# Other points in the quads for decoding weights in a fused attention and two-layer MLP kernel

## The chip, the cores and the metric

The kernel runs on one core of a Trainium2 chip. The metric is device time in microseconds (us) of one execution. Engines are named as in the profile: PE is TensorE's matmuls, PEld its weight loads, DVE is VectorE, ACT is ScalarE, POOL is GpSimd, SP is the engine that issues most DMAs.

## The reference, cut to what matters

```python
attn_out = _attn_ref(x, a, B, C)            # chunked linear attention, 4 x 8 x 768 x 32
x = attn_out.transpose(0, 2, 1, 3).reshape(3072, 256)
h = np.maximum(x @ moe_w_in, 0.0);   x = h * h @ moe_w_out       # layer 1: 256 -> 2048 -> 256
h = x @ moe2_w_in                                                # layer 2: 256 -> 2048 -> 256
out = (h * np.clip(h + 3.0, 0.0, 6.0) / 6.0) @ moe2_w_out
```

All in float32.

## The kernel before

**Numbers.** TensorE multiplies operands of a reduced width (float32r). So every float32 operand is kept as a high part, which ScalarE rounds off, and a low part, the rest, which VectorE or GpSimd subtracts; each product is three matmuls (high by high, low by high, high by low). The weights arrive as raw bits and are *decoded* in blocks: block j is 128 x 512 numbers, even j from w_in and odd j from w_out; blocks 2q and 2q+1 serve quad q of a layer.

**Stages.** First the attention, with the first layer's tiles 0 to 3 beside it (`step`, which ends at about 229 us). Then come 32 *quads* (`emit(g, prev)`, g = 0 to 31): g = 0 to 7 are the first layer for tiles 4 and 5, g = 8 to 31 the second layer. A quad takes two token tiles and two blocks of 128 hidden units at once with seven products instead of eight (a Strassen scheme): `p1`, `p2`, `p6`, `p7`, `p5`, `p4`, `p3` into the PSUM banks X, V and Z, and sums of four gate inputs c11, c22, c21, c12.

**What one quad does, in order.** ScalarE copies X aside after p1 (`s1`), after p6 (`u2`) and after p7 (`u3`); the next product into X (p6, p7, p4) has to wait for the copy. VectorE adds: c11 = V + s1, c22 = Z + u3 (the *c22 add*), and, after p3 has been added to Z, c12 = Z + u2. p3 writes the bank that the c22 add reads, so PE can't start p3 before the c22 add is done. Then, in the first layer, relu and square: VectorE does c11 and c12 (L764), ScalarE does c22 and c21 (L749 and L756). ScalarE makes each high part (`ghc`, L772), VectorE each low part (`glc`, L775), and PE multiplies them with the second weights (`second`). c11 is used at the end of its own quad; c22, c21 and c12 in the quad behind (`prev`).

**Order.** Each engine works strictly in the order in which the program is written. Between the quads' own steps lie numbered points, `run(1000 + g, point)`, in the order 0, 1, 6, 2, 3, 5, 4 through a quad, at which side jobs are hung by `at(1000 + g, point, job)`. Point 1 stands ahead of p6, 6 behind the high part of c11, 2 behind `u3`, 5 between square of c22 and relu of c21, 4 at the quad's end. The side jobs here:

- `w1.renew(q)`: the first layer's weights of quad q are added up again (`whole`, VectorE L507, tile `wta..s`) and GpSimd forms four sums of them (`sums`, L500). `w1.both(2q)` then makes high parts (ScalarE L537: `ea`, `ah`) and low parts (GpSimd L544: `ea`, `al`). The tile `wta..s` of one quad lies where an earlier one lay: `whole` waits until the earlier one's last low part is done.
- Second-layer block j: E (`early`, ScalarE L477), B (`begin`, VectorE L481 and L486, tile `lowb`), M (`end`: VectorE L491 `wtb`, for even j GpSimd's four sums L500, then SP's DMA of block j + 2), and H, or F and G (`both`, or its two parts: ScalarE L537 `bh`, `eb`, GpSimd L544 `bl`, `eb`).
- The second layer's token operands: s, h, l (`oper_sum` on GpSimd L674, `oper_high` on ScalarE L685, `oper_low` on VectorE L691).

The plan of the second layer is a string per quad: "5M4" is M of block 4 at point 5.

Of the kernel before, what the change touches and what calls it, by code (L numbers as in the profile page):

```python
# [41 lines left out]
NQ = DFF // (2 * P)  # L42
# [36 lines left out]
def attn_mlp_mlp(ctx: ExitStack, tc, a, bT, cT, bK, x, w1i, w1o, w2i, w2o, yT):  # L79
# [352 lines left out]
    class Weights:  # L432
# [21 lines left out]
        def at(self, q, k, i, n=1):  # L454

            if (self.pre, q) in own:
                return own[self.pre, q][k][:, i:i + n]
            if 4 <= i < 7:
                return self.ext[q][:, i - 4 + 3 * (k == "l"):][:, 0:n]
            d = self.hi if k == "h" else self.lo  # L460
            return d[q][:, i - 3 * (i > 6):][:, 0:n]
# [432 lines left out]
    w1 = w["a"] = Weights(w1i, w1o, "a")  # L894
# [124 lines left out]
    for q in range(NQ - 2):  # L1019
        if q:  # L1020
            at(52 + 2 * q, 0, lambda q=q: w1.both(2 * q - 2))
        at(52 + 2 * q, 0, lambda q=q: w1.renew(q))
    at(1000, 1, lambda: w1.both(2 * (NQ - 3)))
    for q in range(NQ - 2, NQ):
        at(1000 + q - 6, 5, lambda q=q: w1.renew(q))
        at(1001 + q - 6, 1, lambda q=q: w1.both(2 * q))

    for j in range(2):  # L1030
# [2 lines left out]
        at(49 + j, 0, lambda j=j: w2.both(j))  # L1033
    does2 = {"E": w2.early, "B": w2.begin, "M": w2.end, "H": w2.both, "F": lambda j: w2.part(j, 0),
             "G": lambda j: w2.part(j, 1)}
    for g, plan in enumerate(("6E2 2B2 5M2", "2E3 2B3 5M3", "2E4 2B4 5M4", "1F2 1G2 6H3 2E5 2B5 5M5",
# [3 lines left out]
        for d in plan.split():  # L1040
            at(1000 + g, int(d[0]), lambda f=does2[d[1]], j=int(d[2:]): f(j))
# [9 lines left out]
    def operands(g, key, plan):  # L1051
        for dg, p, f, n in plan:
            if f == "s" and key == ("b", NPAIR - 1):
                at(g + dg, p, lambda n=n: later(key, n))
                continue
            at(g + dg, p, lambda f={"s": oper_sum, "h": oper_high, "l": oper_low, "L": by_pool}[f], n=n: f(key, n))
# [6 lines left out]
    operands(1000 + NQ, ("b", 0),  # L1063
# [4 lines left out]
    for p in range(1, NPAIR):  # L1068
# [61 lines left out]
```

## Time and profile before

| | us |
|---|---|
| median of 3 runs (569.37 to 570.31) | 570.16 |
| the profiled execution | 569.82 |
| its span, first to last instruction | 568.1 |
| PE busy in the span | 550.0 (97%) |
| DVE busy | 434.5 (76%) |
| ACT busy | 382.1 (67%) |
| POOL busy | 194.2 (34%) |

The granted clock is 1.00 from 40 us to the last slice. To read it: with PE busy nearly throughout, the interesting places are the few at which it isn't. The quads have 45 matmuls each (quad 0 has 39) and a pace of their own, so a quad that is longer than its neighbours shows a loss. A row by stretch gives its length, the busy us and instructions of PE, PEld, DVE, ACT and POOL, the granted clock, the DMA engines' share and GB/s. Quads 0 to 7 start at 228.96, 239.23, 249.49, 259.69, 269.90, 280.11, 290.33 and 302.63 us.

### The profile page before, as it was taken

The numbers are of one execution on the slowest core, as the hardware profiler recorded it, in microseconds if no ns is written. First come the engines' busy times: TensorE is split into PE (matmuls) and PEld (weight loads), VectorE is DVE, ScalarE is ACT, GpSimd is POOL, SyncE is SP. The second block draws the span as 40 slices with busy tenths as digits, with TensorE's granted clock in tenths as the row PEclk, the third lists the DMA queues.
The fourth block names the chain that finished last, engine by engine and source line by source line (L and its number), as shares of the span: only waits on it lengthen the run. The fifth ranks groups of instructions, "written<-read, shape, count | busy, mean of one in ns | idle before, by whom it ended". The sixth has DMA issues, their size and how long they took to land.

```text
span 568.1 us, 10494 instructions
## 1 busy us (share of the span) xinstructions
PE 550.0 (97%) x4110; PEld 441.9 (78%) x4110; DVE 434.5 (76%) x668; ACT 382.1 (67%) x692; POOL 194.2 (34%) x262
## 2 busy tenths in 40 slices
PE   7699999999999999999998999999999999999996
PEld 4466777787877888788887888778888888888884
DVE  8687778665554788897899988988867788776774
ACT  5486878454344666767877977778766678666664
POOL 3464442320000787676786705651001500000000
PEclk9899999999999999999999999999999999999999
DMA  7897444223000200112121112000200000200002
GB/s 210 204 244 178 123 141 120 61 65 103 1 2 1 75 0 2 37 38 70 42 75 38 37 41 71 0 2 0 75 0 2 1 2 0 75 0 1 0 2 74
DMA packets 26481, 31.43 MB, mean 55 GB/s; under 512 B 2144, under 2 KB 21056, under 8 KB 26432
## 3 DMA queue, kind: packets, MB, share of 16 engines
q1 hardware_dynamic: 24528, 29.85, 19.0%
q10 hardware_dynamic: 1904, 0.92, 0.6%
q8 instruction: 32, 0.52, 0.4%
q14 instruction: 17, 0.14, 0.1%
HBM read 27.41 MB, written 3.35 MB: 54 GB/s over the span
## 4 chain that ended last, share of the span: by engine, by line
PE 73%; DVE 8%; POOL 8%; ACT 4%; issue 3%; DMA 3%; SPq 1%; ACTq 0%; POOLq 0%; DVEq 0%
PE y L788 26%; PE X L732 13%; PE ya L616 10%; PE ha L582 10%; PE Z L732 6%; PE V L732 3%; DVE glc L775 2%; DMA ef<-scr 2%; DVE c L741 1%; PE att L363 1%; POOL ea L544 1%; DVE wtb L491 1%; DVE c L766 1%; PE att L331 1%; POOL bc L295 1%
## 5 line engine op out<-in xcount | busy, mean ns | idle before, releaser
L775 DVE TENSOR_TENSOR glc<-c,ghc 128x512 fp32r<-128x512 f32 x128 | 97.1, 765 | 7.9 <-ACT ghc L772 7.1
L772 ACT ACTIVATE ghc<-c 128x512 fp32r<-128x512 f32 x128 | 77.9, 629 | 2.7 <-DVE c L766 1.7
L788 PE MATMUL y<-glc,bh 128*128 128x512 f32 x192 | 75.1, 391 | 0.1
L788 PE MATMUL y<-ghc,bh 128*128 128x512 f32 x192 | 74.8, 390 | 0.0
L788 PE MATMUL y<-ghc,bl 128*128 128x512 f32 x192 | 74.7, 389 | 0.0
L766 DVE SCALAR_TENSOR_TENSOR c<-rc,c 128x512 f32<-128x512 f32 x72 | 52.4, 728 | 21.7 <-ACT rc L752 21.7
L599 DVE TENSOR_TENSOR gla<-ga,gha 128x512 fp32r<-128x512 f32 x64 | 50.0, 781 | 23.7 <-ACT gha L597 23.2
L752 ACT ACTIVATE rc<-c,three 128x512 f32<-128x512 f32 x72 | 51.9, 721 | 23.8 <-DVE c L741 23.8
L597 ACT ACTIVATE gha<-ga 128x512 fp32r<-128x512 f32 x64 | 40.6, 635 | 36.4 <-DVE ga L595 36.0
L589 ACT ACTIVATE ga<-ha 128x512 f32<-128x512 f32 x64 | 37.9, 592 | 32.0 <-PE ha L582 32.0
L741 DVE TENSOR_TENSOR c<-Z,u 128x512 f32<-128x512 f32 x64 | 44.0, 687 | 19.8 <-PE Z L732 19.1
L595 DVE TENSOR_TENSOR ga<-ga,ha 128x512 f32<-128x512 f32 x48 | 32.9, 685 | 33.4 <-ACT ga L589 33.0
L737 ACT COPY u<-X 128x512 f32<-128x512 f32 x64 | 37.5, 586 | 26.3 <-PE X L732 26.1
L616 PE MATMUL ya<-gha,ah 128*128 128x512 f32 x128 | 52.4, 410 | 0.0
L582 PE MATMUL ha<-act_h,ah 128*128 128x512 f32 x128 | 51.0, 400 | 0.4 <-ACT ah L522 0.4
L582 PE MATMUL ha<-act_h,al 128*128 128x512 f32 x128 | 50.9, 399 | 0.4 <-POOL al L524 0.3
L616 PE MATMUL ya<-gha,al 128*128 128x512 f32 x128 | 50.4, 394 | 0.0
L582 PE MATMUL ha<-act_l,ah 128*128 128x512 f32 x128 | 50.1, 393 | 0.0
L616 PE MATMUL ya<-gla,ah 128*128 128x512 f32 x128 | 50.0, 390 | 0.0
L544 POOL TENSOR_TENSOR bl<-wtb,bh 128x256 fp32r<-128x256 f32 (+1 forms) x34 | 30.9, 933 | 43.5 <-ACT bh L537 43.5
L788 PEld LDWEIGHTS y<-glc,bh 128*128 128x128 f32 x192 | 36.0, 188 | 8.9 <-DVE glc L775 1.7
L788 PEld LDWEIGHTS y<-ghc,bh 128*128 128x128 f32 x192 | 36.0, 188 | 7.7 <-ACT ghc L772 0.4
(296 smaller groups left out, 1242.7 us busy)
## 6 DMA issues: line engine op xcount, KB each, us to landing
rawa<-in_w1i SPq DMA_DIRECT2D x8, 512.0 KB
rawa<-in_w1o SPq DMA_DIRECT2D x8, 512.0 KB
rawb<-in_w2i SPq DMA_DIRECT2D x8, 512.0 KB
rawb<-in_w2o SPq DMA_DIRECT2D x8, 512.0 KB
xb<-in_x SPq DMA_DIRECT2D x24, 128.0 KB
ef<-scr SPq DMA_DIRECT2D x10, 256.0 KB
out_yT<-xf SPq DMA_DIRECT2D x10, 256.0 KB
bc<-in_cT SPq DMA_DIRECT2D x6, 256.0 KB
```

The source lines that it names most:

```text
L582: nc.tensor.matmul(out=h, lhsT=wt[fb][:, k, fo * P:fo * P + P], rhs=xt[t][:, k, :], start=i == 0, stop=i == 5)
L589: nc.scalar.activation(out=g, in_=h, func=AF.Relu)
L597: nc.scalar.activation(out=gh, in_=g, func=AF.Copy)
L599: nc.vector.tensor_tensor(out=gl, in0=g, in1=gh.bitcast(F32), op=ALU.subtract)
L616: nc.tensor.matmul(out=ys[m], lhsT=terms[i][0][fb][:, fo, m * P:m * P + P], rhs=terms[i][1], start=first and i == 0, stop=last and i == 2)
L732: nc.tensor.matmul(out=self.ps[bank], lhsT=lhsT, rhs=rhs, start=start and i == 0, stop=stop and i == 2, skip_group_check=True)
L741: nc.vector.tensor_tensor(out=self.sb[c], in0=self.ps[bank], in1=self.sb[n], op=ALU.add)
L752: nc.scalar.activation(out=self.sb["r" + c], in_=src, func=AF.Relu, bias=three)
L766: nc.vector.scalar_tensor_tensor(out=self.sb[c], in0=self.sb["r" + c], scalar=6.0, in1=src, op0=ALU.min, op1=ALU.mult)
L772: nc.scalar.activation(out=self.gh[c], in_=self.sb[c], func=AF.Copy)
L775: nc.vector.tensor_tensor(out=self.gl[c], in0=self.sb[c], in1=self.gh[c].bitcast(F32), op=ALU.subtract)
L788: nc.tensor.matmul(out=ys[t][m], rhs=terms[i][1], lhsT=w[self.pre].at(self.q, terms[i][0], 7 + 2 * (1 - f) + m)[:, 0], start=first and i = ...
```

## The change

The program computes the same; only points are other ones. For the first layer's weights, `both(10)` goes from point 1 of quad 0 to point 5, `renew(6)` from point 5 to 4, and `both(12)` from point 1 of quad 1 to point 6. For the second layer's blocks, E2 and E4 go from point 6 to point 2; blocks 5 to 8 are decoded earlier or at other points; the high parts of b21 and t2 and the low parts of b11 and b21 in quads 5 and 6 change places.

```diff
-    at(1000, 1, lambda: w1.both(2 * (NQ - 3)))
-    for q in range(NQ - 2, NQ):
-        at(1000 + q - 6, 5, lambda q=q: w1.renew(q))
-        at(1001 + q - 6, 1, lambda q=q: w1.both(2 * q))
+    for g, p, f, q in ((0, 5, w1.both, 2 * (NQ - 3)), (0, 4, w1.renew, NQ - 2), (1, 6, w1.both, 2 * (NQ - 2)),
+                       (1, 5, w1.renew, NQ - 1), (2, 1, w1.both, 2 * (NQ - 1))):
+        at(1000 + g, p, lambda f=f, q=q: f(q))
...
-    for g, plan in enumerate(("6E2 2B2 5M2", "2E3 2B3 5M3", "2E4 2B4 5M4", "1F2 1G2 6H3 2E5 2B5 5M5",
-                              "1F4 1G4 6H5 2E6 2B6 5M6", "1E7 1B7 2M7 2E8 6F6 5B8 5M8 4G6", "1H7 6E9 2B9 2F8 5M9 4G8",
+    for g, plan in enumerate(("2E2 2B2 5M2", "2E3 2B3 5M3", "2E4 2B4 5M4 5E5 4B5", "1M5 1F2 1G2 6H3 2B6 4E6",
+                              "1M6 1F4 1G4 6H5 2E7 2B7 5M7", "1F6 1G6 6H7 2E8 2B8 5M8", "1F8 1G8 6E9 2B9 5M9",
...
-             ((-4, 0, "s", "t1"), (-4, 2, "s", "t2"), (-4, 4, "h", "b11"), (-3, 1, "h", "b21"), (-3, 2, "s", "t4"),
-              (-2, 0, "s", "t3"), (-2, 1, "h", "t2"), (-2, 1, "l", "b11"), (-2, 5, "l", "b21"), (-1, 1, "l", "t2"),
+             ((-4, 0, "s", "t1"), (-4, 2, "s", "t2"), (-4, 4, "h", "b11"), (-3, 1, "l", "b11"), (-3, 4, "h", "b21"), (-3, 2, "s", "t4"),
+              (-2, 0, "s", "t3"), (-2, 2, "h", "t2"), (-2, 1, "l", "b21"), (-1, 1, "l", "t2"),
```

ScalarE in quad 0 (s1, u2, u3 are the copies; ea5, ah5 are `both(10)`; oa2b22 a token operand; wtb1 is E2; xf3 the last tile of the stage before). Before:

```order
L737 COPY s10_3038<-X0_3034 128x512
L537 ACTIVATE ea5_3004<-wta5s_3003 128x384
L537 ACTIVATE ah5_1146<-wta5s_3003 128x128
L685 ACTIVATE oa2b22_3058<-xin5_2366 128x512
L737 COPY u20_3063<-X0_3034 128x512
L772 ACTIVATE ghc11_0_3065<-c11_0_3044 128x512
L477 ACTIVATE wtb1_3068<-rawb2_2564 128x512
L628 COPY xf3_3078<-ya3_00_2674 128x512
L628 COPY xf3_3078<-ya3_01_2675 128x512
L737 COPY u30_3084<-X0_3034 128x512
L749 ACTIVATE c22_0_3093<-c22_0_3093 128x512
L756 ACTIVATE c22_0_3093<-c22_0_3093 128x512
```

ScalarE in quad 0 now:

```order
L685 ACTIVATE oa2b22_3053<-xin5_2366 128x512
L737 COPY u20_3058<-X0_3034 128x512
L772 ACTIVATE ghc11_0_3060<-c11_0_3044 128x512
L628 COPY xf3_3071<-ya3_00_2674 128x512
L628 COPY xf3_3071<-ya3_01_2675 128x512
L737 COPY u30_3077<-X0_3034 128x512
L477 ACTIVATE wtb1_3079<-rawb2_2564 128x512
L749 ACTIVATE c22_0_3088<-c22_0_3088 128x512
L756 ACTIVATE c22_0_3088<-c22_0_3088 128x512
L537 ACTIVATE ea5_3004<-wta5s_3003 128x384
L537 ACTIVATE ah5_1146<-wta5s_3003 128x128
L749 ACTIVATE c21_0_3107<-X0_3034 128x512
```

E2 and `both(10)` stand behind all three copies; `both(10)` now stands between the square of c22 and the relu of c21.

GpSimd at the turn of quads 0 and 1 (al5 is the last of `both(10)`; wtb1 the sums of block 2; wta6s those of `renew(6)`). Before:

```order
L544 TENSOR_TENSOR al5_1147<-wta5s_3003,ah5_1146 128x128
L500 TENSOR_TENSOR wta6s_3100<-wta6s_3100 128x128 x4
L500 TENSOR_TENSOR wtb1_3068<-wtb1_3068 128x128 x4
L544 TENSOR_TENSOR ea6_3101<-wta6s_3100,ea6_3101 128x256
L544 TENSOR_TENSOR ea6_3101<-wta6s_3100,ea6_3101 128x128
L544 TENSOR_TENSOR al6_1326<-wta6s_3100,ah6_1325 128x128
```

GpSimd at the same turn now:

```order
L544 TENSOR_TENSOR al5_1147<-wta5s_3003,ah5_1146 128x128
L500 TENSOR_TENSOR wtb1_3079<-wtb1_3079 128x128 x4
L500 TENSOR_TENSOR wta6s_3119<-wta6s_3119 128x128 x4
L544 TENSOR_TENSOR ea6_3120<-wta6s_3119,ea6_3120 128x256
L544 TENSOR_TENSOR ea6_3120<-wta6s_3119,ea6_3120 128x128
L544 TENSOR_TENSOR al6_1326<-wta6s_3119,ah6_1325 128x128
```

The sums of the first layer's weights now stand second, behind those of block 2. On VectorE the step that feeds them, L507 `wta6s`, stood right behind the c22 add of quad 0, and now stands behind that quad's `glc22`.

VectorE from the c12 mult of quad 2 to the c22 add of quad 3 (lowb5 and lowb6 are B of blocks 5 and 6, wtb2 is M of block 5). Before:

```order
L764 SCALAR_TENSOR_TENSOR c12_2_3325<-c12_2_3325 128x512
L741 TENSOR_TENSOR c11_3_3352<-V3_3344,s13_3342 128x512
L775 TENSOR_TENSOR glc21_2_3349<-c21_2_3320,ghc21_2_3348 128x512
L764 SCALAR_TENSOR_TENSOR c11_3_3352<-c11_3_3352 128x512
L775 TENSOR_TENSOR glc12_2_3361<-c12_2_3325,ghc12_2_3360 128x512
L775 TENSOR_TENSOR glc11_3_3381<-c11_3_3352,ghc11_3_3380 128x512
L481 TENSOR_SCALAR lowb5_3399<-rawb5_3218 128x512
L486 TENSOR_SCALAR lowb5_3399<-rawb5_3218 128x512
L741 TENSOR_TENSOR c22_3_3406<-Z3_3402,u33_3396 128x512
L491 SCALAR_TENSOR_TENSOR wtb2_3291<-wtb2_3291,lowb5_3399 128x512
```

VectorE from quad 2 to quad 3 now (B of block 5 stands ahead of the c12 mult):

```order
L481 TENSOR_SCALAR lowb5_3333<-rawb5_3218 128x512
L486 TENSOR_SCALAR lowb5_3333<-rawb5_3218 128x512
L764 SCALAR_TENSOR_TENSOR c12_2_3326<-c12_2_3326 128x512
L741 TENSOR_TENSOR c11_3_3356<-V3_3348,s13_3346 128x512
L775 TENSOR_TENSOR glc21_2_3353<-c21_2_3321,ghc21_2_3352 128x512
L764 SCALAR_TENSOR_TENSOR c11_3_3356<-c11_3_3356 128x512
L491 SCALAR_TENSOR_TENSOR wtb2_3291<-wtb2_3291,lowb5_3333 128x512
L775 TENSOR_TENSOR glc12_2_3365<-c12_2_3326,ghc12_2_3364 128x512
L775 TENSOR_TENSOR glc11_3_3388<-c11_3_3356,ghc11_3_3387 128x512
L481 TENSOR_SCALAR lowb6_3405<-rawb6_3318 128x512
L486 TENSOR_SCALAR lowb6_3405<-rawb6_3318 128x512
L741 TENSOR_TENSOR c22_3_3412<-Z3_3408,u33_3403 128x512
```

Block 5's B and M, of which M stood behind the c22 add of quad 3, now both stand ahead of it, with block 6's B in the place of block 5's.

## Rows read from the trace of the kernel before

**Rows 1.** The page's first line.

```profile
span 568.1 us, 10494 instructions
```

**Rows 2.** Quads 0, 3, 5, 6: stretch, length, then busy time by engine.

```profile
228.96:239.23 10.27, 9.39 (x40) 7.09 (x39) 8.51 (x13) 7.52 (x15) 6.30 (x11) 1.00 0.16 51
...
259.69:269.90 10.21, 10.21 (x46) 8.45 (x45) 8.39 (x12) 7.62 (x15) 7.10 (x8) 1.00 0.16 47
...
280.11:290.33 10.22, 10.22 (x46) 8.45 (x45) 9.93 (x15) 8.79 (x18) 7.50 (x9) 1.00 0.22 63
290.33:302.63 12.30, 10.69 (x47) 8.29 (x45) 12.27 (x15) 8.46 (x16) 11.02 (x12) 1.00 0.25 78
```

**Rows 3.** Timeline of PE: start, length, work, [idle before <- who ended it].

```profile
233.80 0.97 PE L732 MATMUL X<-oa2t,ea 128*128 128x512 f32 x3
...
236.34 0.50 PE L732 MATMUL X<-oa2t,ah 128*128 128x512 f32 x1 [0.88 <-ACT u L737]
...
300.46 0.96 PE L732 MATMUL Z<-oa2b,ea 128*128 128x512 f32 x3 [1.61 <-DVE c L741]
```

**Rows 4.** Timeline of ACT in quad 0.

```profile
232.03 0.53 ACT L537 ACTIVATE ea<-wta5s 128x384 fp32r<-128x384 f32 x1 [1.42 <-POOL wta5s L500]
...
234.18 0.66 ACT L477 ACTIVATE wtb<-rawb 128x512 f32<-128x512 f32 x1
...
235.68 0.60 ACT L737 COPY u<-X 128x512 f32<-128x512 f32 x1
```

**Rows 5.** Timeline of DVE in quads 0 to 2: c22 adds, L507, glc22.

```profile
236.32 0.69 DVE L741 TENSOR_TENSOR c<-Z,u 128x512 f32<-128x512 f32 x1 [0.19 <-ACT u L737]
236.93 0.68 DVE L507 TENSOR_TENSOR wta6s<-ah,al 128x512 f32<-128x512 f32 x1
...
239.37 0.79 DVE L775 TENSOR_TENSOR glc<-c,ghc 128x512 fp32r<-128x512 f32 x1 [0.56 <-ACT ghc L772]
...
246.47 0.67 DVE L741 TENSOR_TENSOR c<-Z,u 128x512 f32<-128x512 f32 x1
...
249.51 0.79 DVE L775 TENSOR_TENSOR glc<-c,ghc 128x512 fp32r<-128x512 f32 x1 [0.51 <-ACT ghc L772]
```

**Rows 6.** Timeline of POOL in quads 0 and 1.

```profile
232.63 1.69 POOL L544 TENSOR_TENSOR ea<-wta5s,ea 128x256 fp32r<-128x256 f32 x2 [0.63 <-ACT ea L537]
...
237.69 2.80 POOL L500 TENSOR_TENSOR wta6s<-wta6s 128x128 f32<-128x128 f32 x4 [2.94 <-DVE wta6s L507]
...
243.59 2.06 POOL L544 TENSOR_TENSOR ea<-wta6s,ea 128x256 fp32r<-128x256 f32 x2
245.62 0.64 POOL L544 TENSOR_TENSOR al<-wta6s,ah 128x128 fp32r<-128x128 f32 x1
```

**Rows 7.** Timeline of DVE from quad 2's c22 add to quad 3's.

```profile
256.02 0.69 DVE L741 TENSOR_TENSOR c<-Z,u 128x512 f32<-128x512 f32 x1
...
259.13 0.89 DVE L775 TENSOR_TENSOR glc<-c,ghc 128x512 fp32r<-128x512 f32 x1
...
261.32 0.69 DVE L741 TENSOR_TENSOR c<-V,s 128x512 f32<-128x512 f32 x1 [0.69 <-PE V L732]
...
263.12 2.38 DVE L775 TENSOR_TENSOR glc<-c,ghc 128x512 fp32r<-128x512 f32 x2
...
266.93 0.66 DVE L741 TENSOR_TENSOR c<-Z,u 128x512 f32<-128x512 f32 x1
```

**Rows 8.** Timeline of DVE: quad 5's glc22 and quad 6's c22 add.

```profile
290.79 0.68 DVE L775 TENSOR_TENSOR glc<-c,ghc 128x512 fp32r<-128x512 f32 x1
...
299.73 0.67 DVE L741 TENSOR_TENSOR c<-Z,u 128x512 f32<-128x512 f32 x1
```

**Rows 9.** Groups by line in quads 0 to 7: xcount, busy, mean ns, idle before.

```profile
L491 DVE SCALAR_TENSOR_TENSOR wtb<-wtb,lowb 128x512 uint32<-128x512 uint32 x8 | 6.3, 785 | 0.1
...
L486 DVE TENSOR_SCALAR lowb<-rawb 128x512 uint16<-128x512 uint16 x9 | 5.9, 658 | 0.3
L481 DVE TENSOR_SCALAR lowb<-rawb 128x512 uint32<-128x512 uint32 x9 | 5.9, 654 | 0.0
```

## The prediction

> **What bounds the kernel now.** I read the busy times by quad first, then PE's timeline where a quad is too long, then the timelines of the engines that PE waits for. A quad of 45 matmuls takes 10.21 us when nothing is late (quads 3 and 5) [rows 2]. PE loses time at two places that the change touches. In quad 0, p4 starts at 236.34 behind 0.88 us of waiting for ScalarE's copy u3 [rows 3]; quad 0 has 39 matmuls, 8.85 us at that pace, and takes 10.27: 1.4 us lost. In quad 6, p3 waits 1.61 us for VectorE's c22 add [rows 3], and the quad takes 12.30: 2.1 us lost [rows 2]. In the first, ScalarE is late because its copies stand behind decoding work; in the second VectorE is, which is busy 12.27 of 12.30 us [rows 2].
>
> So VectorE's order has to be read as a cycle. From one quad's c22 add to its glc22 there is a *gap* of some 3.0 us (246.47 to 249.51 [rows 5], 256.02 to 259.13 [rows 7]): ScalarE must do relu, square, relu of c21 and the high part first, so VectorE can fill the gap with the c12 add, an M or an L507, and would idle else. From glc22 to the next c22 add runs a *row* with no room in it: seven steps of the gates and whatever decoding stands there. In quad 2 to 3 that row takes 7.80 us, 0.69 of it waiting for PE [rows 7]; in quad 5 to 6, with block 9's B and the low part of b11 in it and GpSimd busy 11.02 of 12.30 us beside it, 8.94 [rows 2, 8]. Gap and light row are 10.1 us, PE's quad 10.21: the cycle is nearly full already, and a step put into a row costs PE time, while one in a gap costs nothing.
>
> **The change, part by part.** The sum is made against the profiled execution: 569.82 us, span 568.1 [rows 1]; it lies 0.34 below the median of the three runs, 570.16, and the 1.7 us outside the span stay.
>
> *Quad 0.* E2 (0.66) and `both(10)`, which waited 1.42 us for GpSimd and took ScalarE's time from 232.03 [rows 4], now stand behind u3. Then u3 waits only for p7 (233.80 + 0.97 [rows 3]) and takes 0.60: done at 235.4 instead of 236.3 [rows 4], and a little earlier yet since p7 itself waited for u2. p4 gains 0.9 to 1.1; I take 1.0.
>
> *Quad 1.* What was taken away stands elsewhere. `both(10)` is now between square of c22 and relu of c21, so the gap becomes 3.0 + 0.6 = 3.6 us; with the c22 add at 235.2 (236.32 [rows 5] less 1.1), glc22 starts at 238.9 instead of 239.37. L507 of `wta6s`, which lay in the gap (236.93 [rows 5]), stands behind glc22 and waits there for the last low part of `both(10)`: ScalarE's ea ends at about 237.7, GpSimd needs 1.69 [rows 6] and a small last one, to 239.6 or so. It costs the row 0.6 to 0.9. The row was 7.10 (239.37 to 246.47 [rows 5]), so the c22 add of quad 1 comes at 238.9 + 7.8 = 246.7, against 246.47. GpSimd gives the same: two sets of sums at 2.80 [rows 6] from 239.6 end at 245.2, then ScalarE's high parts of `both(12)` (0.6) and u3 (0.6), which is queued behind them, end at 246.4. PE, 1.0 ahead, waits for both: the gain of quad 0 is gone at p3 of quad 1. Given back: 1.0 (0.7 to 1.4).
>
> *Quad 2.* L507 of `wta7s` waits for GpSimd's al6: high parts from 245.2, then 2.06 and 0.64 [rows 6], that is 248.4. Behind it on VectorE are M3, the c12 add and glc22: 248.4 + 3 x 0.6 = 250.2, against 249.51 [rows 5]. The row behind it was 6.51 (249.51 to 256.02 [rows 5, 7]): c22 add at 256.7 against 256.02. PE's p3 comes 36 matmuls, 8.16 us, behind a quad's start, here 257.65, and the add ends at 257.4: no loss, but VectorE's reserve is gone.
>
> *Quad 3.* E5 lies at point 5: the gap is 3.1 + 0.5 = 3.6, glc22 at 260.3. The row loses its 0.69 of waiting and takes on block 5's B and M beside block 6's B. L481 and L486 average 0.65 and 0.66, L491 0.79 [rows 9]; with the overlap of neighbours I count 1.5 to 2.0 for the three, and take 1.5, since GpSimd rests for a part of it. 260.3 + 7.1 + 1.5 = 268.9 for the c22 add against 266.93 [rows 7], its end 269.55. PE wants p3 at 259.69 + 8.16 = 267.85 [rows 2]: lost 1.7 (1.2 to 2.1).
>
> *Quad 4.* M6 is in the row, but GpSimd has nothing to do until M6 is done, so the steps ahead of it are short. 3.0 + 7.0 to 7.4 against 10.21: lost 0.1 (0 to 0.4). M6's four sums now stand in front of blocks 4 and 5 on GpSimd and push its work about 3 us later, into the next rows.
>
> *Quads 5 and 6.* In quad 5 the row has b11's low part and B8, in quad 6 b21's low part (before in the gap) and B9: the same steps as the row of 8.94 [rows 8]. If GpSimd is as busy, each cycle is 3.0 + 8.94 = 11.95, a loss of 1.75 each, 3.5 together. The other end is the row of quad 2 to 3, 7.1 with one B, and 0.6 for the low part: 10.7 with the gap, with 0.2 to spare from quad 4 a loss of 0.4 for both. GpSimd's queue (M6's sums, blocks 4 to 7, two token sums, M8's sums) is nearer to the first: I take 2.6. Gone is quad 6's loss: 2.1.
>
> The DMAs move with M. SP issues block 4 when block 2 has been read, which is earlier, and block 5 at M3, 10 us ahead of its E5; they cost nothing.
>
> Sum: -1.0 + 1.0 + 1.7 + 0.1 + 2.6 - 2.1 = +2.3 us, 572.1. With every end low -0.9, with every end high +4.4.
>
> One rule bears on the 2.6. Two low parts beside GpSimd's work take 2.38 us [rows 7], one without it 0.68 [rows 8]: some 0.5 us more a step. The Trainium skill (SBUF — State Buffer, section "SBUF: two separate sides") says that a VectorE step with two SBUF inputs and a GpSimd step take a shared pair of ports as an exclusive lock, each for its whole length. By that rule nothing is shared, and behind a GpSimd queue that is never empty every such step in a row pays the 0.5; this is the last of the rivals, and by it the sum would be +4.7 where the measured row gives +2.3.
>
> **The rivals.**
>
> *It does what it says* (0.19). Both losses go and nothing takes their place: -1.0 - 2.1 = -3.1, 566.7; with part of quad 1's bill paid, 567 to 568.6. For it: VectorE idles in quads 2 to 4 (0.69 for PE alone [rows 7]), and its busy time there is 8.39 of 10.21 [rows 2]. Against it: the idle time lies in the gap. It decides at quad 3: the c22 add would have to end by 267.85, with the three added steps no longer than 0.5 in all.
>
> *The rows stay light* (0.22). GpSimd's work falls into VectorE's gaps, quads 4 to 6 run at PE's pace, quad 3 loses 1.2 to 1.7: -1.0 + 1.0 + 1.4 + 0.4 - 2.1 = -0.3, 569.5, with 568.9 to 570.7 around it. For it: quad 4 to 5 had two decoding steps in its row without a loss. Against it: GpSimd's queue, which in quad 6 took 11.02 us [rows 2].
>
> *GpSimd's queue is never empty* (0.08). From M6 on each of the rows of quads 5 and 6 then has its ten steps at their length without GpSimd, some 5.7 us (eight starts 0.6 apart, B's two 0.45), and 0.5 on eight of them: 9.7, a cycle of 12.7, 2.5 lost in each. -1.0 + 1.0 + 1.7 + 0.1 + 5.0 - 2.1 = +4.7, 574.5. Block 8's high part on ScalarE, which now stands ahead of u2 in quad 6 and waits for M8's sums, would be late as well. For it: two low parts in 2.38 [rows 7]. Against it: GpSimd itself waits for ScalarE's high parts. It decides where M8's sums end later than about 297. The rule of the Trainium skill above is this case.
>
> **How the numbers follow.** The forecast has 0.51; I count its ends to the rivals, below +0.9 to the light rows and above +4.2 to the full queue. A measurement of this kernel can tell about 0.2%, 1.1 us, from no change. Slower by more: the forecast but for its low end, and the full queue, 0.56. Within: the light rows and that low end, 0.25. Faster: 0.19. The range from 568.2 to 574.0 leaves out the larger part of the first rival (0.12) and the last (0.08); the forecast's own is 570.7 to 574.0.
>
> **What would show it.** Right: p4 of quad 0 at about 235.3 with a wait under 0.3; p4 or p3 of quad 1 waiting about 1 us; L507 of `wta7s` starting near 248.4 behind an idle VectorE; p3 of quad 3 waiting 1 to 2 us for the c22 add, then p3 of quads 5 and 6. Wrong: quad 3 at 10.2 us; quads 4 to 6 all at 10.2; a VectorE idle in rows, waiting for PE. Then VectorE had more room than the cycle shows.

## The result and the profile after

The changed kernel takes 573.47 us in the median of 4 runs (573.07 to 574.36), the kernel before on the same chip 569.81 (569.37 to 570.31): a ratio of 1.0062 with a 95% interval of 1.0044 to 1.0080, or 2.5 to 4.6 us slower. The profiled execution took 573.86 us, with this first line [rows 1]:

```profile
span 572.1 us, 10496 instructions
```

The quads tell where. Quad lengths are differences between the starts of their first matmuls in PE's timeline; the last column runs from quad 0's start to the end of the span.

| | 0 | 1 | 2 | 3 | 4 | 5 | 6 | quad 0 to end |
|---|---|---|---|---|---|---|---|---|
| before | 10.27 | 10.26 | 10.20 | 10.22 | 10.22 | 10.20 | 12.30 | 339.14 |
| after | 9.31 | 11.99 | 10.20 | 11.60 | 10.21 | 12.38 | 11.98 | 343.25 |
| change | -0.96 | +1.73 | 0 | +1.38 | 0 | +2.18 | -0.32 | +4.11 |

From quad 7 on no quad differs by more than 0.05 us, so these changes, 4.00 us together, are nearly all of it. The window view of after, for quads 0, 1, 3, 5 and 6 (columns as in [rows 2]):

```profile
228.85:238.16 9.31, 9.31 (x41) 7.17 (x39) 7.63 (x12) 7.00 (x14) 3.21 (x6) 1.00 0.15 44
238.16:250.15 11.99, 10.98 (x47) 8.14 (x46) 10.39 (x14) 7.92 (x17) 10.00 (x16) 1.00 0.14 39
260.35:271.95 11.60, 10.53 (x47) 8.37 (x45) 9.96 (x14) 7.50 (x15) 7.42 (x8) 1.00 0.15 45
...
282.16:294.54 12.38, 10.81 (x47) 8.29 (x45) 11.39 (x13) 8.16 (x17) 12.38 (x13) 1.00 0.14 40
294.54:306.52 11.98, 10.65 (x47) 8.29 (x45) 10.89 (x13) 8.64 (x17) 8.65 (x10) 1.00 0.14 44
```

In quad 5 GpSimd is busy 12.38 of 12.38 us, where before it had 7.50 of 10.22 [rows 2], and VectorE is busy 11.39. PE's waits from quad 0 on are now these, where before there were two [rows 3]:

```profile
243.08 0.50 PE L788 MATMUL y<-glc,ah 128*128 128x512 f32 x1 [0.82 <-DVE glc L775]
...
247.24 0.50 PE L732 MATMUL X<-oa2t,ah 128*128 128x512 f32 x1 [0.19 <-ACT u L737]
...
269.74 0.98 PE L732 MATMUL Z<-oa2b,ea 128*128 128x512 f32 x3 [1.07 <-DVE c L741]
...
289.14 0.50 PE L788 MATMUL y<-glc,ah 128*128 128x512 f32 x1 [0.24 <-DVE glc L775]
...
292.35 0.96 PE L732 MATMUL Z<-oa2b,ea 128*128 128x512 f32 x3 [1.32 <-DVE c L741]
...
304.36 0.96 PE L732 MATMUL Z<-oa2b,ea 128*128 128x512 f32 x3 [1.33 <-DVE c L741]
```

Each is charged to the c22 add, to a low part ahead of it in VectorE's row, or to u3. A wait costs more than its idle time: the six add up to 4.97 us, while the four quads they stand in are 7.15 us longer than 10.20 each. In quad 5 the idle time is 1.56, and PE's busy time is 10.81 instead of 10.2 for the same matmuls. Part of this is how the rows count. A matmul lasts 0.39 us in them, but the next one starts 0.23 behind it when nothing is late, so the first 0.16 us of a wait count as busy, and a shorter wait shows no idle time at all. The other part is that the matmul behind a wait is followed only after 0.34 us (243.08, then 243.42).

VectorE's steps that the prediction named, with some of their neighbours, in quads 0 to 2, then 2 to 3, then 4 to 5:

```profile
235.24 0.69 DVE L741 TENSOR_TENSOR c<-Z,u 128x512 f32<-128x512 f32 x1
...
238.91 0.97 DVE L775 TENSOR_TENSOR glc<-c,ghc 128x512 fp32r<-128x512 f32 x1 [1.23 <-ACT ghc L772]
239.80 0.95 DVE L507 TENSOR_TENSOR wta6s<-ah,al 128x512 f32<-128x512 f32 x1
240.68 0.95 DVE L764 SCALAR_TENSOR_TENSOR c<-c 128x512 f32<-128x512 f32 x1
...
247.22 0.69 DVE L741 TENSOR_TENSOR c<-Z,u 128x512 f32<-128x512 f32 x1 [0.47 <-ACT u L737]
248.21 0.69 DVE L507 TENSOR_TENSOR wta7s<-ah,al 128x512 f32<-128x512 f32 x1 [0.30 <-POOL al L544]
...
260.28 0.69 DVE L775 TENSOR_TENSOR glc<-c,ghc 128x512 fp32r<-128x512 f32 x1 [0.40 <-ACT ghc L772]
...
264.10 1.22 DVE L491 SCALAR_TENSOR_TENSOR wtb<-wtb,lowb 128x512 uint32<-128x512 uint32 x1
...
269.02 0.67 DVE L741 TENSOR_TENSOR c<-Z,u 128x512 f32<-128x512 f32 x1
...
281.78 0.86 DVE L775 TENSOR_TENSOR glc<-c,ghc 128x512 fp32r<-128x512 f32 x1
282.56 1.22 DVE L764 SCALAR_TENSOR_TENSOR c<-c 128x512 f32<-128x512 f32 x1
283.79 0.69 DVE L741 TENSOR_TENSOR c<-V,s 128x512 f32<-128x512 f32 x1
284.39 1.25 DVE L775 TENSOR_TENSOR glc<-c,ghc 128x512 fp32r<-128x512 f32 x1
285.56 1.22 DVE L764 SCALAR_TENSOR_TENSOR c<-c 128x512 f32<-128x512 f32 x1
286.71 1.23 DVE L691 TENSOR_TENSOR ob0b<-xf,ob0b 128x512 fp32r<-128x512 f32 x1
...
291.62 0.67 DVE L741 TENSOR_TENSOR c<-Z,u 128x512 f32<-128x512 f32 x1
```

The row of quads 0 to 1 is 8.31 us (238.91 to 247.22), that of quads 2 to 3 8.74, that of quads 4 to 5 9.84 (281.78 to 291.62). In the last, most steps that take 0.68 elsewhere take 1.22 to 1.25; the c11 add between them, which reads V from PSUM, still takes 0.69. ScalarE in quads 0 and 1, and GpSimd at that turn and in quad 6:

```profile
234.49 0.59 ACT L737 COPY u<-X 128x512 f32<-128x512 f32 x1
...
245.99 0.53 ACT L537 ACTIVATE ea<-wta6s 128x384 fp32r<-128x384 f32 x1 [1.43 <-POOL wta6s L500]
...
246.62 0.56 ACT L737 COPY u<-X 128x512 f32<-128x512 f32 x1
```

```profile
237.75 1.16 POOL L544 TENSOR_TENSOR ea<-wta5s,ea 128x256 fp32r<-128x256 f32 x2 [5.87 <-ACT ea L537]
...
239.28 3.20 POOL L500 TENSOR_TENSOR wtb<-wtb 128x128 f32<-128x128 f32 x4
242.44 3.52 POOL L500 TENSOR_TENSOR wta6s<-wta6s 128x128 f32<-128x128 f32 x4
...
294.16 2.94 POOL L500 TENSOR_TENSOR wtb<-wtb 128x128 f32<-128x128 f32 x4
...
299.35 2.33 POOL L544 TENSOR_TENSOR bl<-wtb,bh 128x256 fp32r<-128x256 f32 x2
```

u3 of quad 0 is done at 235.1, as wanted; u3 of quad 1 stands at 246.62 behind an `ea` that waited 1.43 us for the second set of sums.

### The profile page after: what moved, and what is told of

Its sections match the earlier page's. It is cut to its first block, busy times and chain, and to the rows that moved or that the text cites. A ratio compares the mean times of both kernels' runs of the same rounds, so it can differ in the third digit from the quotient of the medians.

```text
span 572.1 us, 10496 instructions
## 1 busy us (share of the span) xinstructions
PE 551.7 (96%) x4110; PEld 441.0 (77%) x4110; DVE 435.4 (76%) x668; ACT 382.5 (67%) x692; POOL 193.4 (34%) x262
## 4 chain that ended last, share of the span: by engine, by line
PE 66%; DVE 11%; POOL 9%; issue 5%; ACT 4%; DMA 3%; SPq 1%; ACTq 0%; POOLq 0%; DVEq 0%
PE y L788 23%; PE X L732 11%; PE ya L616 10%; PE ha L582 10%; PE Z L732 6%; DVE glc L775 3%; PE V L732 3%; DVE c L741 2%; DMA ef<-scr 2%; POOL ea L544 1%; PE att L363 1%; DVE wtb L491 1%; PE att L331 1%; DVE lowb L481 1%; PE att L350 1%
## 5 line engine op out<-in xcount | busy, mean ns | idle before, releaser
L775 DVE TENSOR_TENSOR glc<-c,ghc 128x512 fp32r<-128x512 f32 x128 | 97.0, 765 | 9.5 <-ACT ghc L772 8.7
L741 DVE TENSOR_TENSOR c<-Z,u 128x512 f32<-128x512 f32 x64 | 44.0, 687 | 22.3 <-PE Z L732 21.1
L595 DVE TENSOR_TENSOR ga<-ga,ha 128x512 f32<-128x512 f32 x48 | 32.9, 686 | 33.6 <-ACT ga L589 33.3
L500 POOL TENSOR_TENSOR wtb<-wtb 128x128 f32<-128x128 f32 x32 | 20.8, 650 | 64.7 <-DVE wtb L491 62.9
```

What stands on the lines that cost most here:

```text
L741: nc.vector.tensor_tensor(out=self.sb[c], in0=self.ps[bank], in1=self.sb[n], op=ALU.add)
L775: nc.vector.tensor_tensor(out=self.gl[c], in0=self.sb[c], in1=self.gh[c].bitcast(F32), op=ALU.subtract)
```

## The experiments

**How they are compared.** In the profiles quad 0 starts anywhere from 227.39 to 230.97 us, whatever is changed behind it, while a quad whose own steps are left alone mostly repeats within 0.05 us. Beside a full GpSimd queue it can differ more: quad 6 takes 11.98 in the changed kernel, and with the same plan 12.05 in e8_no_sums2 and 12.28 in e3_blocks_only. So one execution's time says less than its trace, and I compare quad lengths and the time from quad 0's start to the end, each from one trace; the timed ratio to the kernel before stands beside it.

| | 0 | 1 | 2 | 3 | 4 | 5 | 6 | quad 0 to end | ratio to before (95%) |
|---|---|---|---|---|---|---|---|---|---|
| e1_first_part | 9.31 | 11.98 | 10.20 | 10.22 | 10.23 | 10.19 | 12.30 | 340.02 | 1.0028 (1.0011 to 1.0045) |
| e2_copies_first | 9.66 | 10.25 | 10.20 | 10.24 | 10.23 | 10.20 | 12.27 | 338.53 | 0.9996 (0.9981 to 1.0011) |
| e3_blocks_only | 10.29 | 10.23 | 10.20 | 11.60 | 10.20 | 12.40 | 12.28 | 342.65 | 1.0060 (1.0037 to 1.0083) |
| e4_gap_block5 | 9.31 | 11.97 | 10.20 | 10.20 | 10.20 | 12.35 | 11.99 | 341.91 | 1.0061 (1.0038 to 1.0083) |
| e5_no_gpsimd | 9.30 | 11.98 | 10.20 | 11.58 | 10.20 | 10.20 | 10.20 | 339.34 | 1.0002 (0.9984 to 1.0019) |
| e6_gap_b8_b9 | 9.31 | 11.98 | 10.20 | 11.59 | 10.20 | 10.92 | 11.11 | 340.98 | 1.0035 (1.0019 to 1.0051) |
| e8_no_sums2 | 9.31 | 10.99 | 10.20 | 11.67 | 10.20 | 12.37 | 12.05 | 342.48 | one run |

**The two parts apart.** The first part alone (E2 is the only E that it moves: E4, which the section on the change names beside it, stands at point 2 in both kernels):

```diff
-    at(1000, 1, lambda: w1.both(2 * (NQ - 3)))
...
+    for g, p, f, q in ((0, 5, w1.both, 2 * (NQ - 3)), (0, 4, w1.renew, NQ - 2), (1, 6, w1.both, 2 * (NQ - 2)),
...
-    for g, plan in enumerate(("6E2 2B2 5M2", "2E3 2B3 5M3",
+    for g, plan in enumerate(("2E2 2B2 5M2", "2E3 2B3 5M3",
```

> The kernel before with the first part of the change alone: E2 behind u3, both(10) at point 5 and renew(6) at point 4 of quad 0, both(12) at point 6 of quad 1; the second layer's blocks from E3 on and the token operands stay as before. My theory (the work moved out of quad 0 comes back as a late L507 and late GpSimd sums in quad 1): quad 0 takes 9.3 us instead of 10.27, quad 1 12.0 instead of 10.26, quads 2 to 7 as before, so +0.8 us, 570.6. Rival (part of quad 1's loss in the changed kernel belongs to the blocks that are moved as well): quad 1 under 11.2 us and the time at or under 569.8.

The second part alone (the plan and the operands of the changed kernel, `both` and `renew` and E2 as before):

> The changed kernel with its first part undone: E2 ahead of u3, renew and both where they were before; the moved blocks 5 to 8 and the moved high and low parts of b11, b21 and t2 are kept. My theory (the parts add up): quads 0 and 1 at 10.27 each, quad 3 11.6 us, quads 5 and 6 12.4 and 12.0, quad 4 10.2; +3.2 us, 573.0. Rival (quads 3 to 6 are late only because quad 1 has pushed everything back): quad 3 under 10.8 us and a time under 571.5.

Quads 0 and 1 of e1_first_part are those of the changed kernel to 0.01 us, quads 2 to 6 those of the kernel before: +0.88 us from quad 0 on, and the ratio's interval lies above 1. e3_blocks_only has the other losses, +3.51. The two add up to +4.4 against +4.11; the difference is quad 6, 12.28 here and 11.98 there, for a cause that was not looked into. So quad 1's loss belongs to the first part alone, and quad 3's is no echo of it.

**Quad 0 mended without the bill.** Only the order on ScalarE is changed against the kernel before:

```diff
-    at(1000, 1, lambda: w1.both(2 * (NQ - 3)))
...
                                    (1000, 1, "h", "b22"), (1000, 6, "l", "b22")))
+    at(1000, 1, lambda: w1.both(2 * (NQ - 3)))
...
-    for g, plan in enumerate(("6E2 2B2 5M2",
+    for g, plan in enumerate(("2E2 2B2 5M2",
```

> The kernel before with quad 0's ScalarE mended in another way: both(10) stays at point 1, but behind the high part of b22, and only E2 goes behind u3; renew(6) and both(12) stay where they were, in VectorE's gap and at point 1 of quad 1. My theory (ScalarE has idle time ahead of u2 that both(10) fits into, and nothing that quad 1 needs becomes later): quad 0 about 9.4 us, quad 1 10.3, total -0.9, 568.9. Rival (quad 1 has a bound of its own in GpSimd's two sets of sums or in VectorE's row, so that whatever quad 0 gains is given back): quad 1 over 11 us, 569.8.

Windows of quads 0 and 1 of e2_copies_first:

```profile
230.97:240.63 9.66, 9.44 (x40) 7.17 (x39) 8.51 (x13) 7.57 (x15) 6.60 (x11) 1.00 0.18 49
240.63:250.88 10.25, 10.25 (x46) 8.45 (x45) 9.59 (x13) 7.45 (x16) 8.21 (x12) 1.00 0.18 55
```

Quad 0 gains 0.61 us and quad 1 stays at 10.25. So up to that gain quad 1 has no bound of its own: its c22 add ends at 248.54, 0.25 us before p3 starts. Whether it could take the whole 0.96 is not shown; in e7_both_mended below, quad 0 takes 9.31 and quad 1 10.70. Most of quad 1's loss in the changed kernel is then the price of what was moved in front of it. 0.3 us less than hoped is gained, since `both(10)`'s low parts now lie beside B2 on VectorE (its L481 takes 0.68 instead of 0.41) and p3 waits 0.20 for the c22 add. The timed ratio can't tell 0.6 us from nothing.

**Which of quad 1's two arms.** In the changed kernel without block 2's sums:

```diff
         t = self.wt[j // 2]
+            if self.pre == "b" and j == 2:
+                nc.sync.dma_start(out=t[:, 4:7].rearrange("p s n -> p (s n)"), in_=zero)
+                return
...
+    zero = const.tile([P, 384], F32, tag="zero", name="zero")
+    nc.vector.memset(zero, 0.0)
```

> The changed kernel with block 2's four sums on GpSimd left out (a DMA copies zeros there, so the second layer's numbers are others); they stand ahead of the sums of renew(6) at the turn of quads 0 and 1. Theory with two arms, as in the prediction (PE waits in quad 1 for VectorE, whose row has L507 in it, and for u3, which is queued on ScalarE behind the high parts of both(12) and so behind both sets of sums): the second arm goes, u3 is done at p7's pace, L507 still lies in the row; quad 1 about 11.3 us instead of 11.99. Rival A (GpSimd's queue is all of it): quad 1 at 10.2 to 10.5. Rival B (L507 in the row is all of it): quad 1 at 11.8 or more.

Quad 1 takes 10.99 us. Of its loss of 1.8 over 10.2, 1.0 goes with these sums and 0.8 stays, so neither rival holds, and the theory's 11.3 was 0.3 too long. u3 now comes at 244.01, 6.38 us behind the quad's start instead of 8.46, and no c22 add waits for it; the row is 7.34 (238.38 to 245.72) instead of 8.31, and PE waits only 0.25 us, for glc21, behind L507. The run takes the sums' place in GpSimd's queue and their work beside VectorE's row away at once, so it doesn't part these two.

**A step in the row or in the gap.** The changed kernel, with M5 and B6 behind the c22 add of quad 3:

```diff
-"2E4 2B4 5M4 5E5 4B5", "1M5 1F2 1G2 6H3 2B6 4E6"
+"2E4 2B4 5M4 5E5 4B5", "1F2 1G2 6H3 5M5 5B6 4E6"
```

> The changed kernel, but in quad 3 M of block 5 and B of block 6 stand behind the c22 add, in the gap, instead of ahead of it; nothing else is moved. My theory (a step in the row costs its length, one in the gap nothing, since VectorE idles 1.07 us there for PE): the row of quad 3 shortens by M5's 1.15 and B6's 1.5 us, the c22 add comes at about 266.5, quad 3 takes 10.2 us instead of 11.6, and quad 4 is no longer than it was; -1.4 us against the changed kernel, 572.1. Rival (GpSimd's work beside the row or PE's own pace decides, not the steps' place): quad 3 over 11.2 us and 573.0 or more.

Windows of quads 3 and 4 of e4_gap_block5:

```profile
258.87:269.07 10.20, 10.20 (x46) 8.45 (x45) 9.85 (x15) 8.36 (x16) 6.89 (x8) 1.00 0.17 51
269.07:279.27 10.20, 10.20 (x46) 8.45 (x45) 9.43 (x14) 8.45 (x17) 6.84 (x10) 1.00 0.35 104
```

All of quad 3's loss is gone, quad 4 is as it was, and from quad 0 on the kernel is 1.34 us shorter than the changed one. The c22 add has 0.25 us of idle time ahead of it, for PE: the same steps, a few microseconds later, cost nothing. The timed ratio, 1.0061, doesn't show the 1.3 us; its interval is 1.3 us wide to either side, so here the trace decides.

The same with B8 and B9:

```diff
-"1F6 1G6 6H7 2E8 2B8 5M8", "1F8 1G8 6E9 2B9 5M9"
+"1F6 1G6 6H7 2E8 5B8 5M8", "1F8 1G8 6E9 5B9 5M9"
```

> The changed kernel, but B of block 8 in quad 5 and B of block 9 in quad 6 stand in the gap behind the c22 add instead of in the row; GpSimd's work is the same. My theory (a step costs in the row what it takes there, 1.47 us each; the gap has 0.46 + 0.62 us of idle time in it and takes two steps of a B at a price of some 0.5): quad 5 about 11.4 us instead of 12.4, quad 6 about 11.0 instead of 12.0; -2.0 us against the changed kernel. Rival (GpSimd's queue sets how long row and gap last together, wherever VectorE's steps stand): quads 5 and 6 still 12.2 and 11.8 or more, no gain.

Quads 5 and 6 fall by 1.46 and 0.87 us, 2.3 together. The row of quads 4 to 5 is shorter by B8's 1.48 (8.36), while the gap behind it grows from 3.05 to 3.94, since M8 and B8 don't fit beside the c12 add. The gap is free only as far as its idle time goes.

**GpSimd beside the row.** The changed kernel without GpSimd's work in quads 4 to 6 (one place of the edit's four is shown):

```diff
                     m = min(2, i0 + m0 - i)
+                    if self.pre == "b" and 4 <= j <= 8:
+                        nc.sync.dma_start(out=self.at(q, "l", i, m).bitcast(F32).rearrange("p s n -> p (s n)"),
+                                          in_=zero[:, 0:m * P])
+                        continue
                     nc.gpsimd.tensor_tensor(out=self.at(q, "l", i, m), in0=self.wt[q][:, i:i + m],
```

> The changed kernel with GpSimd's work of quads 4 to 6 left out: the low parts of blocks 4 to 8, the four sums of blocks 6 and 8 and the first pair's token sums of the second layer are replaced by copies of zeros that DMAs make, so the second layer's numbers are others; every step of VectorE, ScalarE and PE stays. Theory of contention (VectorE's steps in these rows are long because GpSimd's queue is never empty beside them): the steps of 1.22 to 1.25 us fall to 0.6 to 0.7, the rows of quads 5 and 6 from 9.84 and 8.96 to 6.5 to 7.5 us, quads 4 to 6 take 10.2 each, and the time from quad 0's start falls by 3.9 us, to about 569.5 in all; quad 3 stays at 11.6, since its row is left as it was. Rival (the number of steps in the row decides, GpSimd matters little): the rows stay at 8.7 or more, quads 5 and 6 at 11.2 or more each.

Windows of its quads 5 and 6:

```profile
281.32:291.52 10.20, 10.20 (x47) 8.45 (x46) 7.78 (x14) 8.73 (x17) 0.00 (x0) 1.00 0.53 170
291.52:301.72 10.20, 10.20 (x47) 8.45 (x46) 7.78 (x14) 8.53 (x16) 0.00 (x0) 1.00 0.28 86
```

VectorE's groups in quads 4 to 6 (count, busy us, mean ns of one, idle before), after first, then e5_no_gpsimd, whose lines L691, L741, L764 and L775 are 11 or 13 further down:

```profile
L775 DVE TENSOR_TENSOR glc<-c,ghc 128x512 fp32r<-128x512 f32 x12 | 11.3, 956 | 1.3 <-ACT ghc L772 1.2
L764 DVE SCALAR_TENSOR_TENSOR c<-c 128x512 f32<-128x512 f32 x6 | 6.0, 998 | 0.0
...
L691 DVE TENSOR_TENSOR ob0b<-xf,ob0b 128x512 fp32r<-128x512 f32 x2 | 2.5, 1226 | 0.0
L481 DVE TENSOR_SCALAR lowb<-rawb 128x512 uint32<-128x512 uint32 x3 | 2.3, 773 | 0.0
...
L741 DVE TENSOR_TENSOR c<-V,s 128x512 f32<-128x512 f32 x3 | 2.1, 692 | 0.3 <-ACT s L737 0.3
```

```profile
L788 DVE TENSOR_TENSOR glc<-c,ghc 128x512 fp32r<-128x512 f32 x13 | 8.9, 685 | 0.7 <-ACT ghc L785 0.6
...
L777 DVE SCALAR_TENSOR_TENSOR c<-c 128x512 f32<-128x512 f32 x6 | 4.1, 686 | 0.0
...
L754 DVE TENSOR_TENSOR c<-V,s 128x512 f32<-128x512 f32 x3 | 2.1, 692 | 2.1 <-PE V L745 1.8 <-ACT s L750 0.3
...
L702 DVE TENSOR_TENSOR ob0b<-xf,ob0b 128x512 fp32r<-128x512 f32 x2 | 1.4, 686 | 0.0
L481 DVE TENSOR_SCALAR lowb<-rawb 128x512 uint32<-128x512 uint32 x3 | 1.3, 422 | 0.0
```

With the same steps at the same points, quads 5 and 6 run at PE's pace. The row of quads 4 to 5 is 6.94 us, 0.90 of it waiting for PE, against 9.84. So the number of steps is no loss by itself; a light row has room for the three steps of decoding and operands beside its seven. The loss of quads 5 and 6 takes both, these steps in the row and GpSimd's work beside them: the low parts of b11 and b21 (L691, L702) take 686 ns without that work and 1226 with it, and e6_gap_b8_b9, which leaves GpSimd's work as it is, gains 2.3 of the 4.0 us by the place of two steps.

**A version that beats both.** Four versions of the kernel before with e2_copies_first's quad 0 (e7_both_mended with B2 in the gap as well: quad 0 is 0.35 us shorter for it, quad 1 0.45 longer). Since block 9 serves quad 12 first, it can leave quad 6's row.

> Meant to beat both: the kernel before with quad 0's copies first (as in e2_copies_first, and B of block 2 in the gap as well), and block 9 moved out of quad 6 into quad 7's gap (M at its end), block 10 into quad 8's gap, with the high and low parts of blocks 9 to 11 one or two quads later. My theory (quad 6 loses time for the steps in its row alone, and later quads have idle time): quad 0 9.3 us, quad 6 10.2 to 10.5 instead of 12.30, all later ones 10.2; -2.9 us, 566.7. Rival (the load only moves: quad 8's VectorE is already busy 9.6 of its 10.2 us): quad 8 or 9 over 11 us and the time 568.5 or more.

> Meant to beat both: quad 0 as in e2_copies_first (B of block 2 back in the row), block 9 in quad 7's gap, block 10's B in quad 8's gap and its M in quad 9's, block 11 in quad 9's gap behind it with M at the quad's end, the high and low parts of blocks 10 and 11 in quad 10, so that nothing stands in the rows of quads 8 and 9, and GpSimd's work from quad 11 on is as in the kernel before. My theory: quads 0 and 1 together 19.9 us, quad 6 10.5, quads 9 to 14 as in the kernel before, in all 2.2 us less from quad 0's start than the kernel before, 567.6. Rival (quads 9 and 10 lose what quad 6 gains, since VectorE's gap there is no longer than 3 us): quad 9 or 10 over 10.8 us, 568.8 or more.

> e9_later_blocks with one thing changed: in quad 10 the high and low parts of block 10 stand behind u3 and in the gap (points 2 and 5) instead of ahead of u2, and those of block 11 at the quad's end. My theory (quad 10 of e9_later_blocks lost 1.76 us because u2 stood behind those high parts on ScalarE and VectorE's row beside their low parts on GpSimd): quad 10 at 10.2 to 10.4, the rest as in e9_later_blocks; from quad 0's start 2.3 us less than the kernel before, 567.4. Rival (M of block 11 in quad 10's row and the longer gap of quad 9 are the cause): quad 10 still over 11.3 us, no gain on the kernel before.

> The last version meant to beat both: quads 0 to 8 as in e10_later_blocks2; M of block 10 stands late in quad 9's row (point 6) instead of in its gap, block 11 in quad 9 as in the kernel before (B in the row, M in the gap), the high and low parts of block 10 at the end of quad 9 and behind u3 of quad 10, those of block 11 in quad 10's gap. My theory (quad 10 of e10_later_blocks2 lost 0.8 us because M of block 11 stood ahead of the c21 and c12 steps that PE's second products wait for; a light row takes one more step where it comes behind them): quads 9 and 10 at 10.2 to 10.5, quad 11 at 10.2 to 10.4; from quad 0's start 2.0 us less than the kernel before, 567.8. Rival (VectorE has no room for one more block in quads 8 to 10 at any point): quads 9 to 12 lose 1.2 us or more together, and the time is that of e10_later_blocks2.

| | 0 and 1 | 6 | 8 to 14 against before | quad 0 to end | ratio to before (95%) |
|---|---|---|---|---|---|
| before | 20.53 | 12.30 | 0 | 339.14 | |
| e7_both_mended | 20.01 | 10.52 | +1.28 | 338.30 | 0.9980 (0.9966 to 0.9993) |
| e9_later_blocks | 19.86 | 10.53 | +1.81 | 338.54 | 0.9995 (0.9982 to 1.0008) |
| e10_later_blocks2 | 19.86 | 10.50 | +1.43 | 338.29 | 0.9987 (0.9972 to 1.0001) |
| e11_later_blocks3 | 19.89 | 10.48 | +0.34 | 337.08 | 0.9961 (0.9946 to 0.9975) |

Quad 6 gained 1.8 us each time, and the question was where the block's steps went. The first three versions fell well short of the 2.2 to 2.9 us expected of them; the reasons are read from their rows. In e7_both_mended M10 lay ahead of the c12 step in quad 9 (10.70), and the low parts of block 11 pushed GpSimd's token sums into the rows of quads 12 and 13 (+0.31 and +1.11, of which quad 14 gives 0.68 back). In e9_later_blocks quad 10 took 11.96: u2 stood behind the high parts of block 10 on ScalarE. Behind u3 (e10_later_blocks2) quad 10 still took 10.99, for a wait at the second product of c21, which M11 had pushed back, and quads 11 and 12 took 0.68 more together, which was not followed up:

```profile
334.84 0.50 PE L788 MATMUL y<-glc,bh 128*128 128x512 f32 x1 [0.48 <-DVE glc L775]
```

So my theory of e9's loss held for half of it and its rival for the other. With M10 at point 6, behind those steps, e11_later_blocks3 keeps the gain (the plan of quads 6 to 10, against the kernel before):

```diff
-"1H7 6E9 2B9 2F8 5M9 4G8", "1H9 6E10 5B10 4M10", "2F10 5G10", "6E11 2B11 5M11", "2H11 6E12 2B12 5M12"
+"1H7 2F8 4G8", "6E9 5B9 4M9", "2H9 2E10 5B10", "6M10 6E11 2B11 5M11 4F10", "2G10 6E12 2B12 5M12 5H11"
```

Its windows of quads 0, 6 and 10:

```profile
229.62:239.28 9.66, 9.43 (x40) 7.17 (x39) 8.51 (x13) 7.56 (x16) 6.60 (x11) 1.00 0.18 52
...
290.41:300.89 10.48, 10.48 (x46) 8.29 (x45) 9.55 (x12) 7.99 (x15) 10.24 (x12) 1.00 0.13 47
331.49:342.03 10.54, 10.52 (x47) 8.38 (x45) 9.57 (x16) 8.86 (x16) 3.71 (x6) 1.00 0.19 54
```

567.81 us against 570.37 on the same chip: 2.06 us less from quad 0 on, 1.4 to 3.1 by the timed runs.

## Why the prediction was right, and where it was off

The direction and the mechanism held: a cycle of gap and row that was nearly full, with steps put into the row. By its steps:

- *Quad 0, -1.0.* Measured -0.96; p4 starts at 235.13 with no idle time shown. It stands 0.39 behind the matmul ahead of it instead of 0.23, so u3 still holds it a little, and the quad's 9.31 is 0.46 above its pace of 8.85.
- *Quad 1, 1.0 given back.* Measured 1.73: outside the 0.7 to 1.4. The step that failed is a size, that of GpSimd's sums. I took both sets at 2.80 [rows 6]; they took 3.20 and 3.52, and in the kernel before the second set already took more:

```profile
240.44 3.19 POOL L500 TENSOR_TENSOR wtb<-wtb 128x128 f32<-128x128 f32 x4
```

So u3, queued behind them, ended at 247.2 and not 246.4, and p4 starts behind it at 247.24. When nothing is late p4 starts 7.48 us behind its quad (quad 2: 250.15 and 257.63), here at 245.64; these 1.6 us are nearly all of the quad's 1.8 over 10.2. The row came out as forecast: 7.84 us of its 8.31 are steps, against 7.10 plus 0.7, and 0.47 is idle behind u3. PE's wait of 0.82 for glc21 is not in the sum: I followed the c22 add alone, though the row's first steps feed PE as well. It is no loss on top, since PE would otherwise have waited longer for u3. e8_no_sums2 gives 1.0 of the loss to block 2's sums; there u3 is in time, and of the 0.8 that stays PE's wait of 0.25 for glc21 is all that shows as idle time.
- *Quad 2, no loss.* c22 add at 256.69, forecast 256.7; L507 of `wta7s` at 248.21, forecast 248.4.
- *Quad 3, 1.7.* Measured 1.38. glc22 at 260.28 and the c22 add at 269.02 are the forecast's 260.3 and 268.9; PE wanted p3 0.66 later than assumed, since quad 1 had lost that much more. e4_gap_block5 shows that it was M5 and B6 in the row.
- *Quad 4, 0.1.* Measured 0.
- *Quads 5 and 6, 2.6.* Measured 2.18 and 1.78 over 10.2, together 4.0: above the end of 3.5, and 1.4 above the 2.6 that I took. 0.9 of it is the choice of a point below the heavier end; the rest is a mis-sized term, the row of 8.94 taken as that end. Quad 5's is 9.84, which is the 9.7 of the rival with the queue that is never empty, and GpSimd's 12.38 busy us say so; quad 6's is 8.96. For quad 6 the rival's deciding point, M8's sums ending later than about 297, was just met (294.16 + 2.94 = 297.10) and its ScalarE wait didn't come.
- *The sum.* +2.3 forecast, +4.11 in the trace from quad 0 on: 0.7 from quad 1, 1.4 from quads 5 and 6, -0.3 from quad 3, the rest in tenths. Two parts lay outside their own ranges, and the time inside the whole one, near its upper end: that is the width of the range and some luck, not good sizes.

The last of the rivals, with its +4.7, would have been the nearer price. What the runs show: a VectorE step with two inputs in SBUF takes 0.69 us alone and 1.22 to 1.25 beside GpSimd's low parts; a GpSimd low part takes 0.58 alone (1.16 for two) and 1.17 beside VectorE (2.33 for two). Beside low parts, each takes about its own time and the other's. One row was misread on the way there: the step of 0.68 [rows 8] that I took as one without GpSimd's work started at 290.79, with GpSimd at four sums from 290.34 to 293.20. As a length without that work the figure still holds (685 ns in e5_no_gpsimd).

The Trainium skill (SBUF — State Buffer, section "SBUF: two separate sides") calls the shared port pair an exclusive lock, taken for a whole instruction. The trace agrees for the low parts; beside the sums a VectorE step pays only half of a sum's length, as the last section shows.

## What to carry to other kernels

Where one engine's steps run in a cycle with another's, mark which stretch waits (the gap) and which doesn't (the row), and put side work into the gap up to its idle time, behind the steps that feed the bound engine. Cost a step of the row at what it takes with the neighbour engine's queue as it will be, not as it was: here 0.69 or 1.22. Work that is moved out of the way of one wait has to be followed to every engine that it then stands ahead of.

## What the runs showed of the hardware

Steps of VectorE with a PSUM input were not lengthened by GpSimd at all: the c11 add has a mean of 692 ns in both kernels above. Steps with one SBUF input were: L481 422 ns without GpSimd, 773 with it. And the price depends on the neighbour's instruction: beside the sums, which work on 128x128 each, steps took 0.88 to 0.97 (quad 1), beside low parts of 128x256 1.22 to 1.25. A sum takes 0.52 with no VectorE step on two SBUF inputs beside it, as in this row of the changed kernel:

```profile
258.04 2.09 POOL L500 TENSOR_TENSOR wtb<-wtb 128x128 f32<-128x128 f32 x4 [2.03 <-DVE wtb L491]
```

VectorE's steps beside sums start 0.88 us apart (239.80, then 240.68) instead of 0.60 with GpSimd idle (252.39, then 252.99), so each pays 0.28 and not 0.52. Why a sum costs its neighbour half of its length and a low part all of it was not tried.

The whole time varies by nearly 5 us between executions of one kernel, 567.64 to 572.37 for the kernel before, though most quads repeat within hundredths. The rows below, PE's timeline of e2_copies_first and then of e4_gap_block5, show where some of it arises in the first stage, in a place in which the two kernels are the same. Behind the wait of 5.57 us the granted clock was 0.50 from 28.6 to 33.3 us, the lower level of 1.2 GHz; behind the wait of 1.36 it was 1.00. What makes GpSimd's low part come later there was not tried.

```profile
28.61 1.16 PE L331 MATMUL att<-cb,bc 32*64 32x128 f32 x32 [5.57 <-POOL al L524]
```

```profile
24.38 0.70 PE L331 MATMUL att<-cb,bc 32*64 32x128 f32 x32 [1.36 <-POOL al L524]
```
